# First channel product of the last two batches: one Strassen product with seven block products in place of two plain ones

## The chip, the cores and the metric

The kernel runs on one core of a Trainium2 chip. The metric is the device time of one execution in microseconds (us), as the median of several runs. A run's profile is taken in an execution of its own; its times are those of that one execution. TensorE is called PE below (its weight loads PEld), VectorE DVE, ScalarE ACT, GpSimd POOL, and SyncE, which issues most DMA transfers, SP.

## The reference

Eight batches of 576 tokens, eight heads of 64 columns (together 512), float32 in and out. An attention without softmax with a norm is followed by a residual MLP over tokens and over channels:

```
kv  = einsum('bhsd,bhse->bhde', k, v)
o   = einsum('bhsd,bhde->bhse', q, kv)
x   = o / sqrt(mean(o*o, -1) + 1e-6) * g_norm        # then heads side by side: [8, 576, 512]
tok = einsum('ts,bsd->btd', w_tok, alpha1 * x + beta1)
u   = x + lam * tok
a2  = alpha2 * u + beta2
ch  = maximum(a2 @ w_ch1, 0) @ w_ch2                 # 512 -> 2048 -> 512
out = u + lam * ch
```

## The kernel before

**Stages.** The kernel computes one batch after the other in four stages. The 576 tokens are cut into four groups of 128 and a tail of 64; the tails of two neighbouring batches are worked on together, with the odd one of them.

1. attention(b): kv from k and v (PE, L626), then for each token group the product with q (norm, PE, L717) and a chain ACT square L684, DVE reduce L687, ACT root L690, DVE reciprocal L693, DVE multiplications L695 and L702 (into xm, and xt for the tail), POOL multiplication L705 into rm, the input of the token product in bf16.
2. mix(b): the token product tok (L800, four groups of five matmuls with 512 columns, and L845 for the tails), DVE add L810 into xm, POOL cast to bf16 L888 into a2b, and an SP transposing DMA L901 into a2m (a2l for tails). After this a2m holds the batch's activations with channels on the partitions: four blocks of 128 channels by 512 tokens. It has two places, so neighbouring batches stand in it side by side.
3. ch1(b): the first channel product. For each of the 16 blocks of 128 hidden units four matmuls of 512 columns accumulate in one PSUM bank (L911), then ACT adds the bias, takes the maximum with 0 and writes bf16 (relu, L905) into ht, one half of the buffer hh. The tails follow in ch1_tail (L924, relu L941 into hl).
4. The second channel product. Batches 0 and 1 take it plainly (ch2, L967). From batch 2 on it is strassen(b): the [512 tokens x 2048] by [2048 x 512] product is cut into 2 x 2 blocks, and seven block products (L1016, 256 columns each) stand for eight. It needs sums of the blocks of h (DVE, L983, by the helper both, 128x1024 in bf16); its results go out of PSUM by ACT into tmp (keep, L1041) and a POOL addition to xm (L1044), or by a DVE addition straight to xm (last_add, L1049), and are then stored by SP (L1054). The tails have ch2_tail (L1094, L1110) and finish (L1129).

In the program's text the order is, for b from 0 to 7: ch1(b), the tails (odd b), the second product of b, attention(b + 2), mix(b + 2). **What sets the order on the chip** is a table of numbers, ORDER. Each operation has a number, given as it is emitted, and the table lists them in the order in which every engine gets its own instructions; a number behind a colon is the PSUM bank (there are eight), and operations joined by + are woven, matmul by matmul. GATES adds a few dependences. Everything else follows from data: an operation waits for what it reads, and for the readers of what it overwrites. In the table, attention and mix of a batch are spread among the channel products of the batches before it. All of attention(7) and mix(7), tok(7) and the transposes into a2m among it, stand before ch1(6).

**Names that matter.** w1 holds w_ch1 (four blocks of 128 channels by 2048), w2 holds w_ch2, ws1, ws2 and ab_bc are sums of w2's blocks. qs and qp are the buffers into which q is loaded and transposed, wt the token weights, rm the token product's input, sq and tmp scratch tiles of 128x512 f32 (three each). PSUM tiles are called ps. The profile leaves the numbers of buffers out, so w there is w1 or w2.

Of the kernel before, what the change touches and what calls it, by code (L numbers as in the profile page):

```python
# [1407 lines left out]
```

## Time and profile before

| | |
|---|---|
| time, median of 3 runs | 333.48 us (333.26 to 334.75) |
| the profiled execution: time | 335.96 us |
| the profiled execution: span of the core | 333.4 us |
| PE, DVE, ACT, POOL busy | 324.5, 226.5, 176.0, 146.5 us |
| L911 matmuls, 128x512 | 123.3 us busy, 495 seen of 512 |
| L1016 matmuls, 128x256 | 44.4 us, 384 |
| L705 on POOL, L1044 on POOL | 37.9 us and 23.2 us |
| L983 sums on DVE, one form (hh<-hh) | 10.0 us, 14 |

A row of the groups gives the line, the engine, the operation, the tile written and the tile read, the shapes, the number of instructions, the busy time in us with the mean in ns, and the idle time ahead of them with what ended it. Matmuls overlap in the pipeline, so the mean of one (383 ns for L911) is longer than the distance from one to the next. A row of the timeline has the start in us, the length in us, and then the same fields; rows of the same line that follow each other are drawn together.

### The profile page before, as it was taken

The page shows a single profiled execution, that of the slowest core. Times are in us where ns is not written, and L with a number is a line of the kernel's source. Part 1 is how long each engine was busy: PE and PEld are TensorE (multiplying, and loading weights), DVE is VectorE, ACT ScalarE, POOL GpSimd, SP SyncE. Part 2 cuts the span into 40 slices and gives each one's busy share as a digit, 9 for nine tenths or more (in the row PEclk, how much of TensorE's full clock was granted, in tenths as well). Part 3 has the DMA queues.
Part 4 walks back from the last instruction along what each step waited for, and adds up shares of the span by engine and source line. Part 5 has one row for each costly group of instructions (what it writes and reads, how often), then busy time and mean ns, then how long its engine had stood idle before and what let it go on. Part 6 is the DMA issues. An engine that isn't in the chain of part 4 may idle for free.

```text
span 333.4 us, 6156 instructions
## 1 busy us (share of the span) xinstructions
PE 324.5 (97%) x2468; PEld 222.2 (67%) x2497; DVE 226.5 (68%) x389; ACT 176.0 (53%) x358; POOL 146.5 (44%) x146
## 2 busy tenths in 40 slices
PE   8899999999999989999999999999999999999996
PEld 7777564454676535786669864786667784784686
DVE  3785178678999996849998387898897411531432
ACT  5753672239544654629842476727671168418512
POOL 3799027999343544533167313661445300130130
PEclk9999999999999999999999999999999999999999
DMA  7999999999952697599006993994300421012004
GB/s 261 324 265 218 214 208 237 174 188 259 192 151 65 129 289 137 111 283 190 1 18 154 303 176 67 237 176 152 65 0 2 110 97 33 0 38 90 0 2 157
DMA packets 108531, 48.14 MB, mean 144 GB/s; under 512 B 82061, under 2 KB 101589, under 8 KB 108504
## 3 DMA queue, kind: packets, MB, share of 16 engines
q1 hardware_dynamic: 81440, 26.24, 33.5%
q0 software_dynamic: 26800, 21.38, 32.8%
q8 instruction: 19, 0.31, 0.4%
q10 hardware_dynamic: 264, 0.14, 0.2%
q14 instruction: 8, 0.07, 0.1%
HBM read 38.82 MB, written 9.44 MB: 145 GB/s over the span
## 4 chain that ended last, share of the span: by engine, by line
PE 75%; DVE 12%; ACT 5%; DMA 4%; issue 2%; POOL 2%; SPq 0%; DVEq 0%
PE ps L911 22%; PE ps L1016 21%; PE ps L800 8%; PE ps L967 7%; PE ps L924 4%; DVE xm L702 2%; PE ps L717 2%; DMA w<-in_moe_w_ch_dram 2%; DVE ps L695 2%; PE ps L626 2%; DVE small L687 2%; PE ps L1110 2%; PE ps L1094 2%; DVE qp L1278 2%; DMA qs<-in_q_dram 1%
## 5 line engine op out<-in xcount | busy, mean ns | idle before, releaser
L911 PE MATMUL ps<-a2m,w 128*128 128x512 bf16 x495 | 123.3, 383 | 1.2 <-DMA w<-in_moe_w_ch_dram 0.5
L911 PEld LDWEIGHTS ps<-a2m,w 128*128 128x128 bf16 x512 | 48.8, 97 | 53.3 <-issue 1.1
L905 ACT ACTIVATE hh<-ps,b 128x512 bf16<-128x512 f32 x96 | 64.4, 686 | 25.1 <-PE ps L911 24.0
L705 POOL TENSOR_TENSOR rm<-xm,la_bc 128x512 bf16<-128x512 f32 x28 | 37.9, 1357 | 65.0 <-DVE xm L702 64.9
L1044 POOL TENSOR_TENSOR xm<-xm,tmp 128x512 f32<-128x512 f32 x18 | 23.2, 1289 | 60.7 <-ACT tmp L1041 60.7
L1016 PE MATMUL ps<-w,hh 128*128 128x256 bf16 x384 | 44.4, 273 | 0.0
L717 PE MATMUL ps<-kvc,qt 128*128 128x128 f32 (+1 forms) x140 | 42.2, 407 | 0.1
L1016 PEld LDWEIGHTS ps<-w,hh 128*128 128x128 bf16 x384 | 37.5, 98 | 6.0 <-issue 0.4
L967 PE MATMUL ps<-w,hh 128*128 128x512 bf16 x138 | 37.0, 385 | 0.1
L626 PE MATMUL ps<-vr,kr 128*128 128x128 f32 x112 | 34.2, 408 | 1.3 <-DVE b L935 1.3
L1049 DVE TENSOR_TENSOR xm<-ps,xm 128x512 f32<-128x512 f32 x24 | 16.5, 686 | 22.7 <-POOL xm L1044 12.9
L800 PE MATMUL ps<-rm,wt 128*128 128x512 bf16 x107 | 29.5, 382 | 1.0 <-POOL rm L705 0.4
L684 ACT ACTIVATE sq<-ps 128x512 f32<-128x512 f32 (+1 forms) x35 | 20.6, 595 | 18.4 <-PE ps L717 18.1
L983 DVE TENSOR_TENSOR hh<-hh 128x1024 bf16<-128x1024 bf16 x14 | 10.0, 718 | 28.9 <-ACT hh L905 22.3
L717 PEld LDWEIGHTS ps<-kvc,qt 128*128 128x128 f32 (+1 forms) x140 | 27.3, 195 | 2.1 <-ACT qt L1281 0.5
L687 DVE TENSOR_REDUCE small<-sq 128x8 f32<-128x512 f32 (+1 forms) x35 | 23.4, 670 | 7.6 <-ACT sq L684 7.5
L888 POOL CAST a2b<-xm 128x512 bf16<-128x512 f32 x24 | 15.5, 648 | 26.0 <-DVE xm L810 26.0
L941 ACT ACTIVATE hh<-ps,b 128x128 bf16<-128x128 f32 x48 | 13.2, 383 | 22.9 <-PE ps L924 20.3
L1041 ACT ACTIVATE tmp<-ps 128x512 f32<-128x512 f32 x18 | 10.8, 600 | 26.0 <-PE ps L1016 25.9
L626 PEld LDWEIGHTS ps<-vr,kr 128*128 128x128 f32 x112 | 22.4, 200 | 3.0 <-DVE b L935 1.8
L695 DVE TENSOR_TENSOR ps<-ps,small 128x512 f32<-128x512 f32 (+1 forms) x35 | 23.9, 692 | 0.5
L905 ACT ACTIVATE hh<-ps 128x512 bf16<-128x512 f32 x32 | 17.6, 597 | 12.4 <-PE ps L911 12.2
(156 smaller groups left out, 528.8 us busy)
## 6 DMA issues: line engine op xcount, KB each, us to landing
out_dram<-xm SPq DMA_DIRECT2D x32, 256.0 KB, 3.0
kr<-in_k_dram POOLq DMA_DIRECT2D x7, 1024.0 KB, 6.5
vr<-in_v_dram POOLq DMA_DIRECT2D x7, 1024.0 KB, 8.1
qs<-in_q_dram SPq DMA_DIRECT2D x24, 288.0 KB, 4.6
w<-in_moe_w_ch_dram POOLq DMA_DIRECT2D x8, 512.0 KB, 9.8
xm<-in_q_dram SPq DMA_DIRECT2D x8, 288.0 KB, 5.7
qs<-in_v_dram SPq DMA_DIRECT2D x4, 288.0 KB, 5.0
w<-in_k_dram SPq DMA_DIRECT2D x4, 288.0 KB, 5.0
```

Source lines behind the costliest of these rows:

```text
L626: P.mm("fill", 128, [lambda e, t=t, c=c, h=h, o=128 * (h % 4): e.matmul(t.ap()[:, o:o + 128], kr4[:, h, c:c + 2, :].rearrange("p c d -> p ...
L684: P.op("ACT", act(n), lambda e: e.activation(sq[rs, s3, 0:nst, :].rearrange("p h e -> p (h e)"), ps(), ACT.Square), r=[t], w=[("sq", s3)])
L687: P.op("DVE", dve(n), lambda e: e.tensor_reduce(out=st, in_=sq[rs, s3, 0:nst, :], axis=AX.X, op=ALU.add), r=[("sq", s3)], w=[("sm", s4)])
L695: P.op("DVE", dve(n), lambda e: e.tensor_tensor(out=grp(ps()), in0=grp(ps()), in1=st[..., None].to_broadcast([rs.stop - rs.start, nst, DH] ...
L705: P.op("POOL", pool(n), lambda e: e.tensor_tensor(out=r, in0=x.rearrange("p h e -> p (h e)"), in1=la, op=ALU.mult), r=xks + ["la"], w=rks)
L717: P.mm("fill", 128, [lambda e, p=p: e.matmul(dst(p), qt[:, p, cs], kvc[:, i, p, :], start=(p == 0), stop=(p == 3)) for p in range(4)], r=[ ...
L800: P.mm("fill", 512, [lambda e, sc=sc: e.matmul(t.ap(), wt[:, sc if sc < 4 else tw(b), 128 * c:128 * c + 128], rsrc(b, sc, al), start=(sc = ...
L905: P.op("ACT", act(512, 0 if f is None else 1), lambda e: e.activation(dst, t.ap(), ACT.Relu, bias=0.0 if f is None else b1[:, f:f + 1]), r ...
L911: P.mm("main", 512, [lambda e, dj=dj: e.matmul(t.ap(), w1[:, dj, 128 * fj:128 * fj + 128], a2m[:, b % 2, dj, :], start=(dj == 0), stop=(dj ...
L967: P.mm("main", 512, [lambda e, fj=fj, t=t, c=c: e.matmul(t.ap(), (ht[:, fj, 128 * c:128 * c + 128] if c < 4 else hl[:, fj, :]), w2[:, fj, ...
L1016: P.mm("main", 256, [lambda e, c=c, fj=fj: e.matmul(t.ap()[:, 256 * c:256 * c + 256], at[:, fj, 128 * c:128 * c + 128], rhs(fj), start=(fi ...
L1044: P.op("POOL", pool(512), lambda e, cs=cs, f=f: e.tensor_tensor(out=X[:, cs, f], in0=X[:, cs, f], in1=two(tmp[:, s]), op=ALU.add), r=xks(c ...
```

## The change

For batches 6 and 7 ch1 is replaced by pair(6, 7). The two batches stand side by side as the column blocks of one right-hand matrix, and w1 is cut into halves of its channels (rows of the right-hand matrix) and of its hidden units: with B11, B21 the two channel halves of batch 6 in a2m and B12, B22 those of batch 7, the product is a 2 x 2 block product. Strassen's scheme (in Winograd's form) takes seven block products for the eight. Each block product has 8 blocks of 128 hidden units with 2 matmuls of 512 columns: 7 x 16 = 112 matmuls (L960 of the changed kernel) for 2 x 64.

- pair_sums makes eight DVE sums of w1's halves (S1 to S4, each in two parts) and four of the activations (T1 to T4, here u and a2m), all 128x1024 in bf16. S1 and S2 lie in qs, S3 and S4 in rm, two of the T in qp, one in wt, and one in a2m in place.
- pair runs in eight turns x of 14 matmuls, where the second half of a turn overlaps the next turn's first. Partial results go out of PSUM three times a turn by an ACT copy with bias into tmp or sq in f32 (kept, L972), and come out as h by three DVE additions of PSUM and such a copy (L982), each followed by a POOL maximum with 0 in place (L984), and by one ACT relu (L912).
- Batch 7's h gets a place of its own, h7, over the first two batch places of xm (batches 4 and 5), since both batches' h now exist together. Its writers wait until the outputs of batches 4 and 5 are stored.
- Both tails' first products and both second products follow: ch1_tails(7), strassen(6), strassen(7), ch2_tail(7). sums, blocks and four take the batch, since batch 7's h lies elsewhere.
- ORDER is a new table from about its 390th word on, and its bank numbers with it. GATES is unchanged.

The functions from strassen on are otherwise moved down by some 100 lines: L1016 is L1122 in the changed kernel, L983 is L1087, L924 is L1022, L1094 is L1201, L1110 is L1217, L800 is L807, L845 is L852, L810 is L817, L1049 is L1156, L1129 is L1236, L888 is L895, L645 is L652, L687 is L694, L695 is L702, L702 is L709, L717 is L724, L1278 is L1385.

```diff
-465 389 488:5 398 487 386 401 477 500:2 387 497 371 368 472:0 489 501 390 474:4 473 467 391 478:7
...
+465 389 488:5 398 487 386 401 477 500:2 387 497 371 368 472:0 489 501 392 474:4 473 467 393 478:7
...
+        h7 = [xm[:, i].rearrange("p c f -> p (c f)").bitcast(BF16).rearrange("p (j t) -> p j t", j=8)
+              for i in range(2)]
...
+        def pair_sums(b, c):
+            S = [x[:, s] for x in (
+                qs[:, 0:2048].bitcast(BF16).rearrange("p (s j t) -> p s j t", s=2, j=2),
+                rm[:].rearrange("p b c f -> p (b c f)").rearrange("p (s j t) -> p s j t", s=2, j=2))
+                for s in range(2)]
+            T = [x.bitcast(BF16).rearrange("p (j t) -> p j t", j=2)
+                 for x in (qp[:, 0, 0:512], qp[:, 1, 0:512])] + [wt[:, 0:2, 0:512]]
+            kb, kc = ([ak(x, i) for i in range(4)] for x in (b, c))
+            B11, B21 = a2m[:, b % 2, 0:2, :], a2m[:, b % 2, 2:4, :]
+            B12, B22 = a2m[:, c % 2, 0:2, :], a2m[:, c % 2, 2:4, :]
+            for h in range(2):
+                f, g = slice(512 * h, 512 * h + 512), slice(1024 + 512 * h, 1536 + 512 * h)
+                lk, hk = ("w1", h), ("w1", 2 + h)
+                both(ALU.add, S[0][:, :, f], w1[:, 0:2, g], w1[:, 2:4, g], [hk], [("s1", h)])
+                both(ALU.subtract, S[1][:, :, f], S[0][:, :, f], w1[:, 0:2, f], [lk, ("s1", h)], [("s2", h)])
+                both(ALU.subtract, S[2][:, :, f], w1[:, 0:2, f], w1[:, 0:2, g], [lk, hk], [("s3", h)])
+                both(ALU.subtract, S[3][:, :, f], w1[:, 2:4, f], S[1][:, :, f], [lk, ("s2", h)], [("s4", h)])
+            both(ALU.subtract, T[0], B12, B11, kb + kc, [("u", 1)])
+            both(ALU.subtract, T[1], B22, T[0], kc + [("u", 1)], [("u", 2)])
+            both(ALU.subtract, B12, B22, B12, kc, kc)
+            both(ALU.subtract, T[2], B21, T[1], kb + [("u", 2)], [("u", 4)])
+            return S, T
+        def pair(b, c):
+            S, T = pair_sums(b, c)
+            kb, kc = ([ak(x, i) for i in range(4)] for x in (b, c))
+            B11, B21 = a2m[:, b % 2, 0:2, :], a2m[:, b % 2, 2:4, :]
+            T3, B22 = a2m[:, c % 2, 0:2, :], a2m[:, c % 2, 2:4, :]
+            lo_w, hi_w = w1[:, 0:2, :], w1[:, 2:4, :]
+            hc = (ht[:, 0:8], ht[:, 8:16])
+            n = [0]
+            at = {}
+            def pairmm(x, key, first, stop, lhs, o, rhs, r):
+                if first:
+                    at[x, key] = P.bank("main")
+                t = at[x, key]
+                P.mm("main", 512, [lambda e, i=i: e.matmul(
+                    t.ap(), lhs[:, i, 128 * x + o:128 * x + o + 128], rhs[:, i, :],
+                    start=(first and i == 0), stop=(stop and i == 1),
+                    skip_group_check=True) for i in range(2)],
+                    r=r, w=[t])
+                return t
+            def kept(t, f):
+                s = n[0] % 6
+                n[0] += 1
+                dst, key = (tmp[:, s], ("tmp", s)) if s < 3 else (
+                    sq[:, s - 3].rearrange("p h e -> p (h e)"), ("sq", s - 3))
+                P.op("ACT", act(512, 1), lambda e: e.activation(
+                    dst, t.ap(), ACT.Identity, bias=b1[:, f:f + 1]), r=[t, ("b1", f)], w=[key])
+                return dst, key
+            def out_of(t, f, z, k):
+                dst = (h7 if z else hc)[f // 8][:, f % 8, :]
+                keys = [(hkey(c if z else b), f, i) for i in range(2)]
+                if k is None:
+                    relu(dst, t, keys, f)
+                    return
+                P.op("DVE", dve(512), lambda e: e.tensor_tensor(
+                    out=dst, in0=t.ap(), in1=k[0], op=ALU.add), r=[t, k[1]], w=keys)
+                P.op("POOL", pool(512, False), lambda e: e.tensor_scalar(
+                    out=dst, in0=dst, scalar1=0.0, scalar2=None, op0=ALU.max), r=keys, w=keys)
+            k1, k2, k5 = {}, {}, {}
+            for z in range(9):
+                x, y = (z if z < 8 else None), (z - 1 if z else None)
+                if x is not None:
+                    h = x // 4
+                    k1[x] = kept(pairmm(x, "a", True, False, lo_w, 0, B11, [("w1", h)] + kb), x)
+                if y is not None:
+                    out_of(pairmm(y, "a", False, False, S[2], 0, T3, [("s3", y // 4)] + kc), y + 8, 1, k5[y])
+                if x is not None:
+                    out_of(pairmm(x, "b", True, True, hi_w, 0, B21, [("w1", h)] + kb), x, 0, k1[x])
+                if y is not None:
+                    out_of(pairmm(y, "c", False, True, S[3], 0, B22, [("s4", y // 4)] + kc), y, 1, k2[y])
+                if x is not None:
+                    k2[x] = kept(pairmm(x, "a", False, False, S[1], 0, T[1], [("s2", h), ("u", 2)]), x)
+                if y is not None:
+                    out_of(pairmm(y, "a", False, True, hi_w, 1024, T[2], [("w1", 2 + y // 4), ("u", 4)]),
+                           y + 8, 0, None)
+                if x is not None:
+                    k5[x] = kept(pairmm(x, "c", True, False, S[0], 0, T[0], [("s1", h), ("u", 1)]), x + 8)
...
+        def ch1_tails(b):
+            for f4 in range(0, 16, 3 if b == 1 else 4):
+                ch1_tail(b, f4, min(3, 16 - f4) if b == 1 else 4)
...
-        A11, A21, A12, A22 = ht[:, 0:8, 0:256], ht[:, 0:8, 256:512], ht[:, 8:16, 0:256], ht[:, 8:16, 256:512]
+        def blocks(b):
+            lh, hh_ = (h7[0], h7[1]) if b == NB - 1 else (ht[:, 0:8], ht[:, 8:16])
+            return [x[:, :, f:f + 256] for x in (lh, hh_) for f in (0, 256)]
...
+            if b == NB - 2:
+                for i in range(2):
+                    alias([("h7", f, z) for f in range(8 * i, 8 * i + 8) for z in range(2)],
+                          [("x", i, c, p) for c in range(4) for p in range(4)])
+                    alias([("u", i + 1)], [("qp", i)])
+                alias([("u", 4)], [(n, i) for n in ("wt", "wtt") for i in range(2)])
+                alias([("s%d" % m, i) for m in (1, 2) for i in range(2)],
+                      [("qs", g) for g in range(4)])
+                alias([("s%d" % m, i) for m in (3, 4) for i in range(2)],
+                      [("r", i, c, p) for i in range(2) for c in range(4) for p in range(4)])
+                pair(b, b + 1)
+                ch1_tails(b + 1)
+                strassen(b)
+                strassen(b + 1)
+                ch2_tail(b + 1)
+                break
```

**First place: PE around tok(7).** Ahead of it before, strassen(5)'s products (L1016) up to tok(7)'s first group (L800; ab_bc holds a sum of w2's blocks):

```order
L1016 MATMUL ps<-w2,hh 128x256 x32
L1016 MATMUL ps<-ws2,hs 128x256 x16
L1016 MATMUL ps<-ab_bc,hh 128x256 x16
L1016 MATMUL ps<-w2,hh 128x256 x24
L800 MATMUL ps<-rm,wt 128x512 x4
```

Ahead of it now, the same products (L1122) up to the same group (L807):

```order
L1122 MATMUL ps<-w2,hh 128x256 x8
L1022 MATMUL ps<-a2l,w1 128x128 x16
L1122 MATMUL ps<-w2,hh 128x256 x24
L1122 MATMUL ps<-ws2,hs 128x256 x8
L1022 MATMUL ps<-a2l,w1 128x128 x36
L1122 MATMUL ps<-ws2,hs 128x256 x8
L1122 MATMUL ps<-ab_bc,hh 128x256 x16
L1122 MATMUL ps<-w2,hh 128x256 x32
L1022 MATMUL ps<-a2l,w1 128x128 x8
L1122 MATMUL ps<-ws1,hh 128x256 x8
L807 MATMUL ps<-rm,wt 128x512 x4
```

The tails (L1022) and 16 more matmuls of strassen(5) have come ahead of tok(7). Behind it before, from its tail part (L845) to the first matmuls of ch1(6) (L911):

```order
L845 MATMUL ps<-rtl,wt 64x512 x2
L1016 MATMUL ps<-w2,hh 128x256 x8
L1016 MATMUL ps<-ws1,hh 128x256 x16
L924 MATMUL ps<-a2l,w1 128x128 x64
L1094 MATMUL ps<-w2,hh 128x256 x4
L924 MATMUL ps<-a2l,w1 128x128 x32
L1094 MATMUL ps<-w2,hh 128x256 x12
L1110 MATMUL ps<-w2,hh 128x256 x8
L911 MATMUL ps<-a2m,w1 128x512 x4
```

Behind it now (L852 is its tail part, qs holds S1 and S2, qp the first two T, rm S3 and S4):

```order
L852 MATMUL ps<-rtl,wt 64x512 x2
L1122 MATMUL ps<-ws1,hh 128x256 x8
L1022 MATMUL ps<-a2l,w1 128x128 x4
L1201 MATMUL ps<-w2,hh 128x256 x12
L960 MATMUL ps<-a2m,w1 128x512 x2
L1201 MATMUL ps<-w2,hh 128x256 x4
L1217 MATMUL ps<-w2,hh 128x256 x8
L960 MATMUL ps<-a2m,w1 128x512 x2
L1217 MATMUL ps<-w2,hh 128x256 x8
L1022 MATMUL ps<-a2l,w1 128x128 x12
L960 MATMUL ps<-qp,qs 128x512 x4
L960 MATMUL ps<-a2m,w1 128x512 x2
```

Of the 64 tail matmuls of ch1_tails(5) only 4 are left behind tok(7), 60 stand ahead of it among strassen(5)'s products; of the 24 matmuls of strassen(5) behind it 8 are left. The tails of batches 6 and 7 (12 of them here) are spread over the pair.

**Second place: DVE behind tok(7).** Before, from tok(7)'s four adds to the first sums of strassen(6):

```order
L810 TENSOR_TENSOR xm<-ps,xm 128x512 x4
L810 TENSOR_TENSOR xt<-ps,xt 128x512
L1049 TENSOR_TENSOR xm<-ps,xm 128x2x256 x2
L983 TENSOR_TENSOR hh<-hh 128x1024
L1129 TENSOR_TENSOR xt<-ps,xt 128x512
L983 TENSOR_TENSOR hh<-hh 128x4x256
```

Now, from the same adds to the first adds out of the pair (L982):

```order
L817 TENSOR_TENSOR xm<-ps,xm 128x512 x4
L817 TENSOR_TENSOR xt<-ps,xt 128x512
L1087 TENSOR_TENSOR rm<-w1 128x2x512
L1156 TENSOR_TENSOR xm<-ps,xm 128x2x256
L1087 TENSOR_TENSOR rm<-w1,qs 128x2x512 x2
L1087 TENSOR_TENSOR rm<-w1 128x2x512
L1087 TENSOR_TENSOR hh<-hh 128x1024
L1087 TENSOR_TENSOR qp<-a2m 128x1024
L982 TENSOR_TENSOR hh<-ps,tmp 128x512
L1087 TENSOR_TENSOR qp<-a2m,qp 128x1024
L1236 TENSOR_TENSOR xt<-ps,xt 128x512
L1087 TENSOR_TENSOR a2m<-a2m 128x1024
```

S3 and S4 (rm) and three T sums (qp, qp, a2m) stand there anew, with one add out of the pair between them; the fourth T sum follows directly.

**Third place: DVE ahead of tok(7).** It begins with the adds of tok(6) (L810, now L817), and the next reductions (L687, now L694) open attention(7)'s chains. Before:

```order
L810 TENSOR_TENSOR xm<-ps,xm 128x512
L645 TENSOR_TENSOR kvc<-ps,kvo 64x4x64
L810 TENSOR_TENSOR xm<-ps,xm 128x512 x3
L687 TENSOR_REDUCE small<-sq 128x8 x2
L693 RECIPROCAL small<-small 128x8
```

Now:

```order
L817 TENSOR_TENSOR xm<-ps,xm 128x512
L1087 TENSOR_TENSOR qs<-w1 128x2x512
L817 TENSOR_TENSOR xm<-ps,xm 128x512
L1087 TENSOR_TENSOR qs<-qs,w1 128x2x512
L652 TENSOR_TENSOR kvc<-ps,kvo 64x4x64 x2
L1087 TENSOR_TENSOR qs<-w1 128x2x512
L1087 TENSOR_TENSOR hh<-hh 128x4x256
L1087 TENSOR_TENSOR qs<-qs,w1 128x2x512
L1087 TENSOR_TENSOR hs<-hh 128x1024
L694 TENSOR_REDUCE small<-sq 128x8 x2
```

S1 and S2 (qs, four sums) stand there anew, and two sums of strassen(5) (hh, hs) have come forward.

More of the change, by code (lines that the diff above doesn't have):

```diff
@@ L168, in _add @@
                     o.deps.add(y)
-                    if not isinstance(key, Bank) and key[0] in ("sm", "tmp"):
+                    if not isinstance(key, Bank) and key[0] in ("sm", "tmp", "hs"):
                         o.raw.add(y)
@@ L974, in ch2, with four @@
                     finish(b, c, t)
-        A11, A21, A12, A22 = ht[:, 0:8, 0:256], ht[:, 0:8, 256:512], ht[:, 8:16, 0:256], ht[:, 8:16, 256:512]
+        def blocks(b):
+            lh, hh_ = (h7[0], h7[1]) if b == NB - 1 else (ht[:, 0:8], ht[:, 8:16])
+            return [x[:, :, f:f + 256] for x in (lh, hh_) for f in (0, 256)]
         B11, B21, B12, B22 = w2[:, 0:8, 0:256], w2[:, 8:16, 0:256], w2[:, 0:8, 256:512], w2[:, 8:16, 256:512]
-        def four(g, m, n):
-            return [("h", fj, n) for fj in range(8 * m + 4 * g, 8 * m + 4 * g + 4)]
+        def four(g, m, n, b=0):
+            return [(hkey(b), fj, n) for fj in range(8 * m + 4 * g, 8 * m + 4 * g + 4)]
         def both(op, out, in0, in1, r, w):
@@ L1360, in bass_transnormer_attn__then__resmlp_affine_kernel @@
             if b % 2:
-                for f4 in range(0, 16, 3 if b == 1 else 4):
-                    ch1_tail(b, f4, min(3, 16 - f4) if b == 1 else 4)
+                ch1_tails(b)
             if b == 1:
```

33 lines of the change are left out of this document (19 added, 14 removed), and 117 rows, old and new, of the table ORDER.

## The prediction

> **What bounds the kernel now.** I read the page first: busy shares, the slices and the chain.
>
> ```profile
> span 333.4 us, 6156 instructions
> PE 324.5 (97%) x2468; PEld 222.2 (67%) x2497; DVE 226.5 (68%) x389; ACT 176.0 (53%) x358; POOL 146.5 (44%) x146
> PEclk9999999999999999999999999999999999999999
> PE 75%; DVE 12%; ACT 5%; DMA 4%; issue 2%; POOL 2%; SPq 0%; DVEq 0%
> ```
>
> TensorE works 97% of the span at a clock that is never below nine tenths, and has three quarters of the chain that ended last. A share can hide stalls, so the stretches of 8 us around the change come next (PE, PEld, DVE, ACT, POOL busy, clock, DMA share, GB/s), then PE's waits (total, times, longest).
>
> ```profile
> 222.00:230.00 8.00, 8.00 (x65) 6.32 (x64) 8.00 (x16) 3.57 (x7) 2.40 (x3) 1.00 0.99 233
> 246.00:254.00 8.00, 8.00 (x74) 6.97 (x73) 7.88 (x11) 3.02 (x6) 3.51 (x3) 1.00 0.01 2
> 262.00:270.00 8.00, 8.00 (x123) 7.72 (x121) 1.74 (x3) 4.33 (x16) 0.61 (x1) 1.00 0.60 175
> 302.00:310.00 8.00, 8.00 (x38) 3.63 (x37) 1.39 (x2) 6.41 (x10) 0.00 (x0) 1.00 0.03 11
> ...
> PE ps L626 <- DVE b L935: 1.3, 1, 1.3
> ...
> PE ps L800 <- POOL rm L705: 0.4, 1, 0.4
> ```
>
> PE is full in each of them, and between 60 and 331 us its named waits are these two, 1.7 us. So a matmul taken away there is time taken away, if nothing new makes PE wait. VectorE has no air left while the attention chains run (8.00, 7.88) and plenty behind (1.74, 1.39); POOL idles from 262 us on. This is where the change puts its work.
>
> **What it removes.** Batches 6 and 7 had 2 x 64 matmuls of 512 columns (L911); now 7 x 16 = 112 (L960 of the changed kernel). Sixteen go. One lasts:
>
> ```profile
> 299.30 13.76 PE L911 MATMUL ps<-a2m,w 128*128 128x512 bf16 x62
> ...
> 300.15 0.69 ACT L905 ACTIVATE hh<-ps,b 128x512 bf16<-128x512 f32 x1 [5.51 <-PE ps L911]
> ...
> 313.10 0.69 ACT L905 ACTIVATE hh<-ps,b 128x512 bf16<-128x512 f32 x1 [0.18 <-PE ps L911]
> ```
>
> The first and last of batch 7's 16 relus stand 12.95 us apart; each follows four matmuls, so one is 12.95/60 = 0.216 us. Gain: 16 x 0.216 = **3.45 us**. The other matmuls keep count, shape and weaving.
>
> **What it adds, in steady state.** One of the eight turns of the pair has 14 matmuls, 3 ACT keeps, 1 ACT relu, 3 VectorE adds from PSUM and 3 POOL maxima with 0.
>
> ```profile
> L1041 ACT ACTIVATE tmp<-ps 128x512 f32<-128x512 f32 x18 | 10.8, 600 | 26.0 <-PE ps L1016 25.9
> L1049 DVE TENSOR_TENSOR xm<-ps,xm 128x512 f32<-128x512 f32 x24 | 16.5, 686 | 22.7 <-POOL xm L1044 12.9
> L888 POOL CAST a2b<-xm 128x512 bf16<-128x512 f32 x24 | 15.5, 648 | 26.0 <-DVE xm L810 26.0
> L1044 POOL TENSOR_TENSOR xm<-xm,tmp 128x512 f32<-128x512 f32 x18 | 23.2, 1289 | 60.7 <-ACT tmp L1041 60.7
> L705 POOL TENSOR_TENSOR rm<-xm,la_bc 128x512 bf16<-128x512 f32 x28 | 37.9, 1357 | 65.0 <-DVE xm L702 64.9
> ```
>
> PE needs 14 x 0.216 = 3.02 us for a turn; ACT at most 4 x 0.69 = 2.76 (the relu's length; a keep has 0.60); VectorE 3 x 0.69 = 2.06. None passes PE. The maximum has no row. Its ends are 0.65 (the cast, one tensor in) and 1.36 (two tensors in), so POOL needs 1.94 to 4.07 us. I take 0.65, since the maximum reads one tensor too. Then PE hides all three, and the term is nothing; with that cover gone it is the last rival's.
>
> By the Trainium skill, page "GPSIMD Engine Reference", section 4.1, an elementwise maximum belongs to VectorE: GpSimd is about half as fast with two inputs and near line rate with one. By that this term stays nothing; no run here shows such a maximum.
>
> **The sums.** Twelve VectorE sums of 128x1024 are new: eight of w1's halves (S), four of the activations (T).
>
> ```profile
> L983 DVE TENSOR_TENSOR hh<-hh,hs x12: 639/992/1799, 138.4 to 317.3; 128x1024 bf16<-128x1024 bf16 x12
> ...
> 289.48 1.32 POOL L1044 TENSOR_TENSOR xm<-xm,tmp 128x512 f32<-128x512 f32 x1 [26.44 <-ACT tmp L1041]
> ...
> 288.39 1.29 DVE L983 TENSOR_TENSOR hh<-hs,hh 128x1024 bf16<-128x1024 bf16 x2
> 289.68 2.27 DVE L983 TENSOR_TENSOR hh<-hh,hs 128x1024 bf16<-128x1024 bf16 x2
> 254.10 1.28 POOL L705 TENSOR_TENSOR rm<-xm,la_bc 128x512 bf16<-128x512 f32 x1 [0.38 <-DVE xm L702]
> ...
> 256.17 0.81 PE L800 MATMUL ps<-rm,wt 128*128 128x512 bf16 x3
> ```
>
> A pair of sums takes 1.29 us alone, 2.27 beside a POOL operation of 1.32 that reads SBUF: 0.64 to 1.80 each.
>
> By the Trainium skill, page "SBUF — State Buffer", section "Who interferes with whom", a VectorE instruction with two SBUF inputs contends with a GpSimd one that reads SBUF, with one such input it doesn't. The 2.27 agrees. By it the adds out of PSUM stay free of the maxima and only sums collide.
>
> Four S sums (into qs) and one last_add come newly ahead of tok(7), where VectorE is full: 4 x 0.64 + 0.69 = 3.2 us, with every sum colliding 4 x 1.80 + 0.69 = 7.9. Before, POOL's last rm ended at 255.38 and PE went into tok(7) at about 256, so delay there would show. But the new order also brings PE work ahead of tok(7): 60 tail matmuls (128 columns) and 16 of strassen(5) (256 columns).
>
> ```profile
> 264.19 3.74 PE L924 MATMUL ps<-a2l,w 128*128 128x128 bf16 x64
> ...
> 267.77 0.60 PE L1094 MATMUL ps<-w,hh 128*128 128x256 bf16 x4
> ...
> 269.99 1.47 PE L1094 MATMUL ps<-w,hh 128*128 128x256 bf16 x12
> 271.30 0.93 PE L1110 MATMUL ps<-w,hh 128*128 128x256 bf16 x7
> ```
>
> 64 tails start 3.58 us ahead of what follows, 0.056 each; 12 of 256 columns 1.31, 0.109 each. So PE comes 60 x 0.056 + 16 x 0.109 = 5.1 us later. The balance is -1.9 to +2.8; I take **nothing**: at the row's median, 0.99, VectorE's share is 4.7 against 5.1.
>
> **The joint behind tok(7)** is the tight place: S3, S4 and T stand between it and their first products.
>
> ```profile
> 257.03 1.03 PE L800 MATMUL ps<-rm,wt 128*128 128x512 bf16 x4
> 258.11 1.03 PE L800 MATMUL ps<-rm,wt 128*128 128x512 bf16 x4
> ...
> 261.56 1.05 PE L1016 MATMUL ps<-w,hh 128*128 128x256 bf16 x8
> ...
> 261.67 0.69 DVE L810 TENSOR_TENSOR xt<-ps,xt 128x512 f32<-128x512 f32 x1 [0.51 <-PE ps L845]
> ...
> 261.22 0.61 POOL L888 CAST a2b<-xm 128x512 bf16<-128x512 f32 x1 [0.47 <-DVE xm L810]
> ...
> 262.49 1.26 SPq L901 DMA_TRANSPOSE a2m<-a2b  x1
> ...
> a2m<-a2b SPq DMA_TRANSPOSE x4, 2.5
> out_dram<-xm SPq DMA_DIRECT2D x4, 256.0 KB, 4.3
> ```
>
> Groups of tok are 1.08 apart, so tok(7) began at 257.03 - 1.08 = 255.95; its tail ended 5.61 later. Count from that start. PE then has 40 matmuls of 256 columns (4.36), 16 tails (0.90) and 4 of the pair (0.86) that need no T: the product with T0 is due at 5.61 + 6.12 = 11.7, that with T1 two matmuls later, 12.2, that with T3 at 13.9 (two more with T, four without, 8 tails). On VectorE xt's add ends at 262.36 - 255.95 = 6.4; then, 0.60 apart as a pair of sums alone has it (1.29 less the 0.69 of one), four S sums, a last_add and a ch2_tail sum: 10.0. The last transpose has landed by then (262.49 - 255.95 + 2.5 = 9.0). So T0 ends at 10.6, an add out and T1 at 11.8, an xt add and T3 at 13.0. Slack: 1.1, 0.4 and 0.9. A POOL cast or maximum in the way takes 0.61 of it, and two stand there. Ends: nothing, and three T sums at 1.80 instead of 0.65, 3.45 less T3's 0.9 = 2.5. I take **+0.5 us**, two collisions (1.22) less a slack between T1's and T3's.
>
> Batch 7's first add goes into xm and waits for batches 4 and 5's stores. Issued by about 10 (the last_add behind S3 ends near 7.6, SP has the transposes ahead), they land 4.3 later, at 14.3; PE gives that add its product at 13.9 + 0.43 = 14.3. Tenths, within the 0.5.
>
> **Sum:** 335.96 (the profiled execution's own time) - 3.45 + 0.5 = 333.0. The median of the runs lies 2.48 below that execution, so **330.5 us**.
>
> **Rivals.**
> *The new order also sheds old waits.* All positions behind about 55 us are new. Then the 1.3 wait may go, the joint may be free: 333.48 - 3.45 - 1.3 = 328.7. For it: the wait stands at one place only. Against: what it waits for may be a load, which an order of instructions doesn't hasten.
> *VectorE is late.* The S sums cost part of 2.8 at tok(7), T part of 2.5 at the joint: either gives up to 330.0 + 2.8 = 332.8, three quarters of both 334.0; I price it at 332.5. For it: 7.88 of 8 busy, and 1.80 seen. Against: POOL works 3.51 of 8 us there, so not all four collide.
> *POOL's maximum costs as with two tensors, slower.* On VectorE, sums that strassen(6)'s third product needs stand behind a sum over batch 7's last maxima. PE would reach that product 24.2 (eight turns) + 2.2 (40 tails) + 3.5 (32 of 256 columns) = 29.9 us after the pair's start; three sums of 0.60 come between, and 0.6 until the first maximum can begin, so 27.5 are left for 24 maxima: up to 1.15 each they hide. At 1.36 they take 32.6: +5.1 and 330.5 + 5.1 = 335.6. The old time is passed from 1.15 + (3.45 - 0.5)/24 = 1.27 each. For it: POOL's commonest rows are at 1.29 and 1.36. Against: those have two tensors in, and the casts 0.65.
> *The change doesn't do what it says*, PE being not the bound: the full windows exclude it.
>
> **How the numbers follow.** My forecast (329.8 to 331.4) has 0.58, the shed waits 0.10 (328.7 to 329.8), late VectorE 0.24 (331.4 to 334.0), slow maxima 0.08 (334 to 336). The range 329.0 to 333.5 leaves out a third of the second, little of the third and the fourth, 0.15 in all. Within 0.5%, about what a measurement can tell from no change, is 331.81 to 335.15. Faster: 0.58 + 0.10 + 0.03 = 0.71; same: 0.21 of the third and 0.02 of the fourth, 0.23; slower 0.06.
>
> **What would show it.** Right: PE full in the pair's windows, its span 3 us shorter from tok(7) to the end, waits on L1087 sums below 1 us in all, maxima near 0.65. Wrong: a PE wait on rm or rtl before tok(7) (the S sums), on qp or a2m at the first T products (the joint), on PSUM banks with POOL busy throughout (the maxima), or a wait at 60 to 250 us that wasn't there (the order).

## The result, and the profile after

The changed kernel takes 348.18 us (median of 4 runs, 345.88 to 349.9) where the kernel before takes 334.12 (median of 4 runs, the three behind the 333.48 above and one more); the ratio is 1.0416, 95% interval 1.0347 to 1.0485. It is 4% slower, and the prediction of 330.5 (329.0 to 333.5) was wrong.

The page of the changed kernel first: span, busy shares, the slices of PE, POOL and the clock, the chain by engine, and the group of the new POOL maxima.

```profile
span 343.7 us, 6215 instructions
PE 326.3 (95%) x2481; PEld 221.2 (64%) x2481; DVE 246.1 (72%) x425; ACT 173.6 (50%) x358; POOL 180.4 (52%) x170
...
PE   7999999999999999999999999799999995949996
...
POOL 3699047998345523723580435533235479994240
PEclk9999999999999999999999999999999999896999
...
PE 73%; POOL 11%; DVE 8%; DMA 4%; issue 2%; ACT 1%; SPq 0%; DVEq 0%
...
L984 POOL TENSOR_SCALAR xm<-xm 128x512 bf16<-128x512 bf16 x16 | 23.9, 1507 | 3.2 <-DVE xm L982 3.2
```

Before, PE's slices had no dip in the last third, and POOL had 2% of the chain. Now POOL has 11%, its slices are full in the stretch of the pair, PE has two dips there, and in the same place the granted clock leaves nine tenths for the first time. One maximum takes 1.5 us. PE's waits from 60 us on (total, times, longest):

```profile
PE ps L960 <- DVE xm L982: 8.8, 2, 5.1
PE ps L1122 <- DVE hs L1087: 2.1, 1, 2.1
PE ps L807 <- DVE rtl L707: 0.2, 1, 0.2
```

Two waits of 8.8 us together lie in the pair, one of 2.1 far ahead of it (217 us); the waits of 1.3 and 0.4 of before are gone. The timeline of PE around the two waits (start, length, what, idle before):

```profile
285.89 1.03 PE L960 MATMUL ps<-qp,qs 128*128 128x512 bf16 x4
290.56 0.69 PE L960 MATMUL ps<-wt,w 128*128 128x512 bf16 x2 [3.64 <-DVE xm L982]
291.04 1.91 PE L960 MATMUL ps<-a2m,w 128*128 128x512 bf16 x4
292.75 1.82 PE L960 MATMUL ps<-a2m,rm 128*128 128x512 bf16 x4
294.41 1.03 PE L960 MATMUL ps<-qp,qs 128*128 128x512 bf16 x4
...
310.18 1.03 PE L960 MATMUL ps<-wt,w 128*128 128x512 bf16 x2 [5.14 <-DVE xm L982]
311.01 5.53 PE L1122 MATMUL ps<-w,hh 128*128 128x256 bf16 x32
316.37 1.80 PE L1122 MATMUL ps<-ws,hs 128*128 128x256 bf16 x15
```

PE waits for VectorE's adds. What holds these shows on VectorE and POOL:

```profile
288.81 1.08 DVE L1087 TENSOR_TENSOR hh<-hh 128x1024 bf16<-128x1024 bf16 x1 [4.29 <-POOL hh L984]
...
308.43 1.09 DVE L1087 TENSOR_TENSOR hh<-hh 128x1024 bf16<-128x1024 bf16 x1 [4.88 <-POOL hh L984]
...
284.40 2.93 POOL L984 TENSOR_SCALAR xm<-xm 128x512 bf16<-128x512 bf16 x2
287.30 1.48 POOL L984 TENSOR_SCALAR hh<-hh 128x512 bf16<-128x512 bf16 x1
```

On VectorE a sum of strassen(6) stands among the adds out of the pair. It waits 4.29 us for the maximum of batch 6's fourth block (POOL, 287.30 + 1.48 = 288.78), all adds behind it wait with it, and PE waits for a bank that they have to free. The same happens at 308 us. VectorE stood idle through those 4.29 us, and the maxima still followed each other every 1.45 us (2.93 less 1.48), so VectorE isn't what slows them.

The second part of the loss is in the lengths: behind the first wait 8 matmuls take 294.41 - 291.04 = 3.37 us, where 8 x 0.216 = 1.73 are due; behind the second 32 of 256 columns take 316.37 - 311.01 = 5.36 for 3.50. That is 1.64 + 1.86 = 3.5 us of slow clock.

So, span against span: 333.4 - 3.45 (16 matmuls) + 8.8 (waits in the pair) + 3.5 (slow clock) + 0.6 (2.1 + 0.2 - 1.3 - 0.4, the waits ahead of it) = 342.9, of 343.7 measured; 0.8 us are left without a name. The spans differ by 10.3 us and the medians by 14.1, because the profiled execution was the fastest of the four now (345.88 us) and above the median before (335.96): the other 3.8 us lie in executions that left no trace.

### The profile page after: what moved, and what is told of

Its sections match the earlier page's. It is cut to its first block, busy times and chain, and to the rows that moved or that the text cites. A ratio compares the mean times of both kernels' runs of the same rounds, so it can differ in the third digit from the quotient of the medians.

```text
span 343.7 us, 6215 instructions
## 1 busy us (share of the span) xinstructions
PE 326.3 (95%) x2481; PEld 221.2 (64%) x2481; DVE 246.1 (72%) x425; ACT 173.6 (50%) x358; POOL 180.4 (52%) x170
## 4 chain that ended last, share of the span: by engine, by line
PE 73%; POOL 11%; DVE 8%; DMA 4%; issue 2%; ACT 1%; SPq 0%; DVEq 0%
PE ps L1122 22%; PE ps L1009 21%; PE ps L807 9%; PE ps L1069 7%; POOL xm L984 6%; PE ps L1022 3%; POOL hh L984 3%; DMA w<-in_moe_w_ch_dram 2%; PE ps L724 2%; PE ps L633 2%; PE ps L1201 2%; DMA w<-in_k_dram 1%; PE ps L852 1%; DVE ps L702 1%; PE ps L1217 1%
## 5 line engine op out<-in xcount | busy, mean ns | idle before, releaser
L1009 PE MATMUL ps<-a2m,w 128*128 128x512 bf16 x384 | 99.4, 385 | 0.5 <-DMA w<-in_moe_w_ch_dram 0.5
L712 POOL TENSOR_TENSOR rm<-xm,la_bc 128x512 bf16<-128x512 f32 x28 | 35.6, 1276 | 60.8 <-DVE xm L709 60.7
L1009 PEld LDWEIGHTS ps<-a2m,w 128*128 128x128 bf16 x384 | 36.3, 97 | 37.8 <-issue 1.1
L912 ACT ACTIVATE hh<-ps,b 128x512 bf16<-128x512 f32 x72 | 48.2, 684 | 17.2 <-PE ps L960 8.9
L724 PE MATMUL ps<-kvc,qt 128*128 128x128 f32 (+1 forms) x140 | 42.0, 405 | 0.0
L1122 PE MATMUL ps<-w,hh 128*128 128x256 bf16 x320 | 38.6, 281 | 0.0
L1069 PE MATMUL ps<-w,hh 128*128 128x512 bf16 x144 | 37.9, 385 | 0.0
L1122 PEld LDWEIGHTS ps<-w,hh 128*128 128x128 bf16 x320 | 32.2, 101 | 5.8 <-issue 0.6
L895 POOL CAST a2b<-xm 128x512 bf16<-128x512 f32 x24 | 16.2, 678 | 34.7 <-DVE xm L817 32.0
L694 DVE TENSOR_REDUCE small<-sq 128x8 f32<-128x512 f32 (+1 forms) x35 | 23.4, 677 | 12.7 <-ACT sq L691 12.3
L1156 DVE TENSOR_TENSOR xm<-ps,xm 128x512 f32<-128x512 f32 x24 | 16.5, 688 | 20.9 <-POOL xm L1151 13.9
L807 PE MATMUL ps<-rm,wt 128*128 128x512 bf16 x112 | 29.4, 380 | 0.6 <-DVE rtl L707 0.6
L724 PEld LDWEIGHTS ps<-kvc,qt 128*128 128x128 f32 (+1 forms) x140 | 27.3, 196 | 1.7 <-ACT qt L1388 0.4
L984 POOL TENSOR_SCALAR xm<-xm 128x512 bf16<-128x512 bf16 x16 | 23.9, 1507 | 3.2 <-DVE xm L982 3.2
L702 DVE TENSOR_TENSOR ps<-ps,small 128x512 f32<-128x512 f32 (+1 forms) x35 | 23.9, 692 | 0.6
L912 ACT ACTIVATE hh<-ps 128x512 bf16<-128x512 f32 x32 | 17.5, 597 | 12.4 <-PE ps L1009 12.2
```

The lines of the kernel that those rows point to most:

```text
L694: P.op("DVE", dve(n), lambda e: e.tensor_reduce(out=st, in_=sq[rs, s3, 0:nst, :], axis=AX.X, op=ALU.add), r=[("sq", s3)], w=[("sm", s4)])
L702: P.op("DVE", dve(n), lambda e: e.tensor_tensor(out=grp(ps()), in0=grp(ps()), in1=st[..., None].to_broadcast([rs.stop - rs.start, nst, DH] ...
L712: P.op("POOL", pool(n), lambda e: e.tensor_tensor(out=r, in0=x.rearrange("p h e -> p (h e)"), in1=la, op=ALU.mult), r=xks + ["la"], w=rks)
L724: P.mm("fill", 128, [lambda e, p=p: e.matmul(dst(p), qt[:, p, cs], kvc[:, i, p, :], start=(p == 0), stop=(p == 3)) for p in range(4)], r=[ ...
L807: P.mm("fill", 512, [lambda e, sc=sc: e.matmul(t.ap(), wt[:, sc if sc < 4 else tw(b), 128 * c:128 * c + 128], rsrc(b, sc, al), start=(sc = ...
L912: P.op("ACT", act(512, 0 if f is None else 1), lambda e: e.activation(dst, t.ap(), ACT.Relu, bias=0.0 if f is None else b1[:, f:f + 1]), r ...
```

## The experiments

Theory 1 is that the price of the POOL maxima is the loss. Its rivals: the pair's own latency or VectorE (theory 2), and the new order (theory 3). Medians are in us; each ratio is against runs of the kernel before on the same chip.

| run | median (range) | before | ratio, 95% interval |
|---|---|---|---|
| max_8_columns | 334.64 (331.42 to 337.06) | 335.23 | 0.9977 (0.9948 to 1.0006) |
| max_on_vector | 333.22 (331.91 to 334.5) | 335.23 | 0.9943 (0.9921 to 0.9964) |
| max_on_vector_old_order | 331.57 (329.36 to 333.32) | 335.23 | 0.9896 (0.9860 to 0.9933) |
| plain_new_order | 342.52 (341.74 to 343.05) | 335.23 | 1.0221 (1.0187 to 1.0254) |
| pool_forms | 335.77 (one run) | 334.95 | none |
| max_416_columns | 342.11 (341.14 to 342.86) | 334.95 | 1.0210 (1.0180 to 1.0239) |
| vector_rm_first | 329.83 (328.61 to 330.76) | 334.95 | 0.9841 (0.9814 to 0.9868) |
| plain_new_order_2 | 337.55 (336.82 to 337.77) | 334.95 | 1.0071 (1.0044 to 1.0098) |
| sums_late | 342.82 (341.53 to 343.38) | 335.27 | 1.0234 (1.0194 to 1.0274) |
| fed_waits | 344.57 (343.01 to 347.05) | 335.27 | 1.0299 (1.0246 to 1.0352) |
| plain_rm_first | 333.51 (332.38 to 336.16) | 335.27 | 0.9963 (0.9935 to 0.9992) |
| vector_rm_first_again | 329.72 (328.87 to 331.09) | 335.27 | 0.9847 (0.9811 to 0.9882) |

### Is it the maximum?

max_8_columns cuts each maximum to its first 8 columns, max_on_vector keeps all of it and changes the engine.

```diff
                 P.op("POOL", pool(512, False), lambda e: e.tensor_scalar(
-                    out=dst, in0=dst, scalar1=0.0, scalar2=None, op0=ALU.max), r=keys, w=keys)
+                    out=dst[:, 0:8], in0=dst[:, 0:8], scalar1=0.0, scalar2=None, op0=ALU.max), r=keys, w=keys)
```

```diff
-                P.op("POOL", pool(512, False), lambda e: e.tensor_scalar(
+                P.op("DVE", dve(512, 4), lambda e: e.tensor_scalar(
```

> The changed kernel with each of the 24 POOL maxima cut from 512 columns to the first 8 (so three quarters of the last two batches' h stay without their maximum); order, banks and all other work are the same. Theory 1, POOL's price: the maxima at 1.48 us are the whole loss; PE's two waits in the pair (8.8 us) go, and with them the slow clock behind them (about 3.7 us): 334.1 - 3.45 - 1.7 (old waits gone) + 2.3 (new waits before the pair) = 331.3 us, range 330 to 333. Theory 2, the pair's own latency (PSUM to ACT copy to VectorE add, and VectorE's sums): PE still waits inside the pair, time above 338. Theory 3, the new order: the loss lies before the pair, time above 338 with no wait inside it.

> The 24 maxima on VectorE, same line, same place in the order; nothing left out. Price from the row of the 128x2048 bf16 tensor_scalar before (803 ns): about 0.2 us each for 512 columns, so VectorE has 3 x 0.69 + 3 x 0.2 = 2.7 us in a turn of 3.02. Theory 1: 331.3 us, range 330 to 333, ratio 0.990 against before, no wait above 1 us in the pair. Theory 2: VectorE is the narrow engine, so its longer queue makes it worse than the 8 columns on POOL by 2 us or more. Theory 3: above 338.

Both take the loss away: 13.5 and 15.0 us below the changed kernel. max_on_vector came 1.9 us above what theory 1 said (1.1 of them stand in the kernel before as well, which took 335.23 there and not 334.12), max_8_columns 3.3 and so outside its range. There the miss goes with the clock: the four of its ten runs with a mean granted clock of 0.999 or 1.000 took 331.4 to 333.4 us, the six with 0.990 to 0.995 took 334.6 to 337.1; where the clock fell in those six no trace shows. Neither profile has a wait in the pair. PE's waits of max_on_vector from 34 us on, and what the maxima cost there (minimum, median, maximum in ns):

```profile
PE ps L1122 <- DVE hs L1087: 2.1, 1, 2.1
PE ps L724 <- ACT qt L1388: 0.9, 1, 0.9
PE ps L807 <- DVE rtl L707: 0.6, 2, 0.4
...
L984 DVE TENSOR_SCALAR xm<-xm x16: 283/284/288, 279.5 to 301.8; 128x512 bf16<-128x512 bf16 x16
```

The same instruction takes 0.28 us on VectorE and 1.48 on POOL. VectorE now has 3 x 0.69 + 3 x 0.28 = 2.9 us of work in a turn of 3.02 and still delays nobody: theory 2 falls. The wait of 2.1 us is still there, and it isn't the maxima's.

### What makes it dear on POOL?

pool_forms puts four forms in the maximum's place, in turn.

```diff
+                form = forms[0] % 4
+                forms[0] += 1
+                if form == 0:
+                    P.op("POOL", pool(512, False), lambda e: e.tensor_copy(out=dst, in_=dst), r=keys, w=keys)
+                elif form == 1:
+                    P.op("POOL", pool(512, False), lambda e: e.tensor_scalar(
+                        out=dst, in0=dst, scalar1=0.0, scalar2=None, op0=ALU.add), r=keys, w=keys)
+                elif form == 2:
+                    P.op("POOL", pool(512, False), lambda e: e.tensor_scalar(
+                        out=dst, in0=la_bc[:], scalar1=0.0, scalar2=None, op0=ALU.max), r=keys, w=keys)
+                else:
+                    P.op("POOL", pool(256, False), lambda e: e.tensor_scalar(
+                        out=dst[:, 0:256], in0=dst[:, 0:256], scalar1=0.0, scalar2=None, op0=ALU.max),
+                        r=keys, w=keys)
```

> The changed kernel with the 24 POOL maxima replaced in turn by four forms, six each, to read their prices: a copy of the bf16 tile onto itself, an addition of 0 in place (tensor_scalar), a maximum with 0 of a float32 tile (la_bc) written as bf16, and the maximum in place on 256 of the 512 columns. It leaves the maximum out for most of the last two batches' h, and replaces a quarter of it by a constant. Known: 1.48 us for the maximum on 512 columns, 0.23 on 8, 0.65 for a cast float32 to bf16. Theory operand type (reading bf16 is slow): copy and addition about 1.48 us, the float32 maximum about 0.65. Theory operation (tensor_scalar is slow): copy about 0.65, addition and float32 maximum about 1.48. Either way 256 columns 0.23 + 248 x 2.48 ns = 0.85.

The POOL groups of its pair (busy us, mean ns): an addition and a float32 maximum by tensor_scalar, 256 columns of the maximum, the casts as before, and the copy.

```profile
L990 POOL TENSOR_SCALAR xm<-xm 128x512 bf16<-128x512 bf16 x4 | 6.0, 1491 | 3.8 <-DVE xm L983 3.8
L996 POOL TENSOR_SCALAR xm<-xm 128x256 bf16<-128x256 bf16 x5 | 4.2, 841 | 0.0
...
L993 POOL TENSOR_SCALAR hh<-la_bc 128x512 bf16<-128x512 f32 x2 | 3.0, 1480 | 0.0
...
L895 POOL CAST a2b<-xm 128x512 bf16<-128x512 f32 x4 | 2.4, 612 | 4.2 <-DVE xm L817 4.2
L988 POOL COPY xm<-xm 128x512 bf16<-128x512 bf16 x3 | 1.8, 606 | 0.0
```

It is the operation, not the type: a tensor_scalar of 512 columns takes 1.48 to 1.49 us for a maximum and for an addition, from bf16 and from float32, about two and a half times a copy or cast (0.61). The prediction had taken the cast's row for it because both read one tensor.

### From which price does POOL decide?

max_416_columns has the edit of max_8_columns with 416.

> The maxima on POOL, cut to 416 of 512 columns (a fifth of those h stay without it): 0.23 + 408 x 2.48 ns = 1.24 us each. The prediction put the point from which POOL decides at 1.15 us: 24 x (1.24 - 1.15) = 2.2 us over max_on_vector's 333.2, with some slow clock 335 to 338. If the decision point is a good deal lower, waits are near the full 8.8 us and the time is above 342; if it is higher, the time is 333.

PE's waits in the pair there:

```profile
PE ps L960 <- DVE xm L982: 5.5, 3, 2.9
```

At 1.24 to 1.29 us per maximum the time was 342.1, and PE waited in the pair 5.5 us, not the 2.2 expected: the decision point lies below the 1.15 of the prediction. Rows of the changed kernel, from POOL and VectorE, bound it:

```profile
277.15 1.49 POOL L984 TENSOR_SCALAR xm<-xm 128x512 bf16<-128x512 bf16 x1 [2.16 <-DVE xm L982]
...
282.64 0.69 DVE L982 TENSOR_TENSOR xm<-ps,tmp 128x512 bf16<-128x512 f32 x1 [1.14 <-PE ps L960]
283.25 0.68 DVE L982 TENSOR_TENSOR hh<-ps,sq 128x512 bf16<-128x512 f32 x1
283.85 0.68 DVE L982 TENSOR_TENSOR xm<-ps,tmp 128x512 bf16<-128x512 f32 x1
```

The waiting sum needs eight maxima from 277.15 on, and VectorE was free for it at 284.5 (the add at 283.85 and its length). Of its 4.29 us of waiting PE felt 3.64, so the banks cover 0.65, and PE waits when the eighth maximum ends behind 284.5 + 0.65 = 285.2. Eight in a row reach that at (285.2 - 277.15)/8 = 1.0 us each. Cheaper ones would not stand in a row, since each must wait for its add: POOL began 0.8 us after the start of an add (277.15 against 276.37), so the last two, for the adds at 282.64 and 283.25, take from 283.4 on, and they reach 285.2 at 0.9 us each. So PE waits from about 0.9 us on. That is an estimate from these rows, and no run lies between 0.23 and 1.1 us; pool_forms, whose four forms have a mean of 1.1 us, had 3.0 us of waits in the pair.

### POOL's throughput, or the place of the sums?

sums_late moves five sums in the order (numbers of the table, what stands between left out): 1522 to 1524 behind the last add out of the pair, 1558 and 1560 behind 1525.

```diff
-... 1522 ... 1558 ... 1523 ... 1524 ... 1483 ... 1560 ... 1525 ...
+... 1483 1522 1523 1524 ... 1525 ... 1558 1560 ...
```

> The changed kernel (maxima on POOL, 512 columns) with five VectorE sums moved in the order: the three of strassen(6) that stood among the adds out of the pair go behind the last of these, the two of strassen(7) behind strassen(6)'s. VectorE then has nothing between its adds that waits for a maximum. Theory POOL's throughput: the waits inside the pair go, but strassen(6)'s first product needs 21 of the maxima, which POOL ends near 306 while PE is there at 301, and its third one waits little more: 5 to 6 us of waits in place of 8.8, and 348.2 - 3.2 = 345 us, some slow clock less. Theory VectorE's order: the sums that waited are the cause, PE's waits fall to under 2 us and the time to 337 or less.

PE's waits from 34 us on:

```profile
PE ps L1124 <- POOL hh L986: 7.0, 1, 7.0
PE ps L1124 <- DVE hs L1089: 2.1, 1, 2.1
```

The waits inside the pair are gone, but one of 7.0 us stands behind it, directly for POOL (5 to 6 were expected), and the time is 342.8 us (345 were expected): 5.4 below the changed kernel, of which the profiled spans show 2.5 (343.7 against 341.2), and 7.5 above the kernel before. 24 maxima at 1.48 are 35.5 us, and eight turns of the pair 24.2, so moving the sums alone left most of the loss; other work of PE behind the pair might cover more, which was not tried. The place of the sums on VectorE decided where the wait appeared and a part of its size.

### The slow clock

fed_waits puts 60 and 88 idle matmuls (their results are used by nothing) ahead of the two that waited, into the banks 6 and 5, which nothing else uses there. Some lines of Python that let an idle matmul name its bank are left out here.

```diff
-... 1427 ... 1488 ...
+... ~60:6 1427 ... ~88:5 1488 ...
```

> The changed kernel with 60 and 88 idle matmuls of 128 columns (0.056 us each) into a free PSUM bank ahead of the two matmuls at which PE waited 3.64 and 5.14 us; nothing else is changed and the waits' causes stay. Theory clock: the slow stretches behind those waits (3.5 us in the profile: 8 matmuls in 3.37 for 1.73, 32 in 5.36 for 3.50) follow from PE's idleness and go: 348.2 - 3.5 = 344.7 us. Rival: the granted clock falls for another reason: 348 or more.

344.57 us, as theory clock had it (344.7). Its waits' causes are unchanged; PE works through most of them (2.5 us of waits are left in the pair), and the windows (the clock is the third number from the end) beside those of the changed kernel show what went. First the changed kernel, then fed_waits:

```profile
288.00:296.00 8.00, 5.44 (x18) 2.07 (x19) 5.33 (x8) 2.33 (x4) 7.29 (x6) 0.79 0.00 0
...
304.00:312.00 8.00, 2.86 (x26) 1.87 (x24) 2.29 (x3) 2.41 (x8) 7.64 (x6) 0.75 0.00 0
312.00:320.00 8.00, 8.00 (x63) 6.54 (x62) 5.90 (x8) 1.64 (x4) 2.34 (x3) 0.82 0.01 2
```

```profile
288.00:296.00 8.00, 5.94 (x47) 3.27 (x46) 6.14 (x9) 3.45 (x6) 7.29 (x6) 1.00 0.00 0
...
304.00:312.00 8.00, 7.55 (x114) 7.14 (x113) 3.45 (x5) 2.47 (x8) 6.85 (x5) 1.00 0.01 2
312.00:320.00 8.00, 8.00 (x75) 7.17 (x74) 5.60 (x8) 1.50 (x3) 4.45 (x3) 1.00 0.00 0
```

With PE kept busy the clock stays at 1.00, so it followed PE's idleness: 3.6 us between the medians came from it, a quarter of the loss (3.5 by the lengths above). The Trainium skill, page "TensorE: Matmul & The Clock Gate", section "HAM oscillation — how this bites in real kernels", says that PE falls back to half its clock behind idle gaps above about 3.4 us. The gaps of 3.64 and 5.14 us agree, and so does the half: 3.37/8 = 0.42 us for a matmul of 0.216. But 3.4 us was not the boundary here. PE behind the longest wait of max_416_columns:

```profile
307.72 1.03 PE L960 MATMUL ps<-wt,w 128*128 128x512 bf16 x2 [2.90 <-DVE xm L982]
308.55 4.94 PE L1122 MATMUL ps<-w,hh 128*128 128x256 bf16 x32
313.32 1.91 PE L1122 MATMUL ps<-ws,hs 128*128 128x256 bf16 x16
```

Behind only 2.90 us, 32 matmuls of 256 columns took 313.32 - 308.55 = 4.77 us where 3.50 are due, while behind a wait of 3.04 us in plain_new_order 32 of 128 columns took the usual 1.80.

### The order

Theory 3 was tried from two sides: plain products in the new order (plain_new_order, and with a mended seam plain_new_order_2), and the pair with cheap maxima in the old one (max_on_vector_old_order). Each takes the one kernel's table up to and with tok(7) and the other's from there on.

> The kernel before (plain products for batches 6 and 7), with the new order up to and with tok(7), restricted to the operations both kernels have, and the order before from there on; no S sums ahead of tok(7). Theory 1: the order before the pair costs little: 334.1 + 2.3 - 1.7 = 334.7, range 333.5 to 336. Theory 3: the new order is the loss: above 340.

> The pair with the maxima on VectorE, but the order before up to and with tok(7); from there the new order, so all eight S sums stand behind tok(7), with 5.1 us more of other PE work there than in the changed kernel. Theory 1: 331.3 less the 0.6 us that the new order costs ahead of the pair, 330.7 us; up to 2.4 us more (four sums of 0.6) if the S sums there come on top. Theory 3: the old order gives all of the loss back, which theory 1 says has nothing to do with it: then this one is below max_on_vector by 5 us or more.

> plain_new_order, whose seam behind tok(7) had a wait of 3.0 us for a transposed tail, with 16 matmuls of ch1(6) moved ahead of the tails that waited. Theory 1 with the order's price seen between the two kernels with the maxima on VectorE (333.2 against 331.6): 335.2 + 1.6 = 336.8, up to 339.5 if only the 3.0 go. Theory 3: the new order itself costs as before, 341 or more.

plain_new_order missed its expectation by 7.8 us and looked like theory 3. A part was the seam itself: the tails taken ahead of tok(7) were missing as cover behind it, and PE waited 3.0 us for a transposed tail. With 16 matmuls of ch1(6) put there it took 337.55, 2.6 us above the kernel before. With the maxima on VectorE the new order takes 333.22 and the old 331.57. So the new order ahead of the pair costs about 2 us, not the 14 of the loss. All kernels of the new order that are shown so far have a wait of 2.1 to 2.2 us near 217. VectorE and POOL of max_on_vector show it:

```profile
212.57 4.04 DVE L1087 TENSOR_TENSOR hh<-hs,hh 128x1024 bf16<-128x1024 bf16 x1
...
212.83 0.70 POOL L1379 DMA_DIRECT2D kr<-in_k_dram  x1
213.53 1.30 POOL L712 TENSOR_TENSOR rm<-xm,la_bc 128x512 bf16<-128x512 f32 x1
214.77 1.28 POOL L1151 TENSOR_TENSOR xm<-xm,tmp 128x512 f32<-128x512 f32 x1
```

A sum took 4.04 us instead of 0.68 and ended at 216.61, only when POOL's multiplication and addition in a row were over (214.77 + 1.28 = 216.05). vector_rm_first moves the multiplication ahead of three DMA issues on POOL:

```diff
-... 1092 ... 1089 ... 1091 ... 1090 ... 1104 ...
+... 1092 ... 1104 1089 1091 1090 ...
```

> max_on_vector with one move in the order: on POOL, one rm multiplication (L712, op 1104) goes ahead of three of the four DMA issues that load k and v (ops 1089 to 1091), near 211 us. There a VectorE sum took 4.04 us and PE waited 2.1 us for its successor. Theory lock: the sum stood behind POOL's two float operations in a row that read SBUF; with rm done before, the sum takes 0.7, PE's wait goes, and with it the slow clock behind it: 333.2 - 2.1 = 331.1 us or up to 1.7 less. Rival: the DMA issues block the sum as well, it stays at 3 us or more and the time at 333.2.

```profile
211.15 1.27 POOL L714 TENSOR_TENSOR rm<-xm,la_bc 128x512 bf16<-128x512 f32 x1
212.36 0.94 POOL L1377 DMA_DIRECT2D kr<-in_k_dram  x1
...
212.17 0.79 DVE L1089 TENSOR_TENSOR hh<-hh 128x1024 bf16<-128x1024 bf16 x1
212.88 0.68 DVE L1089 TENSOR_TENSOR hh<-hs,hh 128x1024 bf16<-128x1024 bf16 x1
```

The sum takes 0.68 beside the DMA issues, PE's wait is gone, and the time is 329.83, 3.4 us below max_on_vector. That is 1.3 more than the wait. The clock accounts for a part of it: in max_on_vector's profile the window 216 to 224 had 0.79, and 24 matmuls of 256 columns behind the wait took 4.29 us where 2.62 are due. But only four of its twelve runs had a mean clock below 1.00, so the rest stays open.

### What the pair itself is worth

plain_rm_first and vector_rm_first_again have one order up to tok(7) and the same move; they differ in the product and what follows.

> plain_new_order_2 (plain products, new order) with the same move as in vector_rm_first. If PE's wait of 2.1 us and the slow clock behind it go here too: 337.5 - 2.1 = 335.4 or up to 1.7 less, 333.7. Beside vector_rm_first (329.8) it gives what the pair with cheap maxima is worth in one and the same order up to tok(7); the count of matmuls says 3.45 us, so by that it is 333.3. If the pair's order behind tok(7) gives more than the matmuls, it is above 334.5.

> vector_rm_first once more, on the same chip as plain_rm_first, so that the two can be set beside each other: 329.8 us again, within 1 us; less plain_rm_first by 3.45 if the matmuls are all of it.

333.51 against 329.72: 3.8 us, where 16 matmuls are 3.45. The two share the chip and the runs of the kernel before. vector_rm_first is the best version: 1.6% below the kernel before (0.9841, 0.9814 to 0.9868, and 0.9847 when run again).

## Why the prediction was wrong, point by point

- **PE is the bound, 16 matmuls are 3.45 us.** Right: plain_rm_first against vector_rm_first_again gives 3.8. That vector_rm_first's 329.8 lies within the predicted range is no success of the forecast: it has the maxima on another engine and one more move in the order.
- **ACT and VectorE are hidden in a turn.** Right, even with 0.28 us more for each add on VectorE (max_on_vector, no wait in the pair).
- **"I take 0.65, since the maximum reads one tensor too."** This is the step that failed. The maximum takes 1.48 us, above both ends of 0.65 and 1.36. The number of inputs was the wrong likeness: a cast and a tensor_scalar read one tensor each and differ by a factor of 2.4 (pool_forms). The sentence on the Trainium skill, page "GPSIMD Engine Reference", section 4.1, leaned the same way with its near line rate for one input; the measurement decides against it for this operation. Its other half, that a maximum belongs to VectorE, is what the runs bear out: 0.28 against 1.48 us.
- **The rival of slow maxima (0.08).** Its mechanism was the one that happened, with sums on VectorE behind late maxima. Its price was not: by its formula 24 x 1.48 - 27.5 = 8.0 us late, 338.5, and the 8.8 us of waits agree with that. What it left out was the slow clock behind such waits (3.5) and the order (below). It also took only the sums behind the pair; the one in its middle decides earlier, near 0.9 us and not at 1.15.
- **S sums ahead of tok(7): nothing.** Right: 0.2 us of wait there. But a sum's worst case was put at 1.80; an old sum in the new order took 4.03, and PE waited 2.1 us. The prediction looked for the new order's cost only where sums were added, not where old ones had moved beside POOL's work.
- **The joint: +0.5 us.** It cost nothing: PE takes tok(7), the tails and the first T products without a wait. T1's sum ended at 273.64, while its product came two matmuls behind 273.57. Batch 7's first add waited for PE, not for the stores.

These rows carry the last point: VectorE's T1 sum and its first add into xm, and PE's first matmuls with T:

```profile
272.96 0.68 DVE L1087 TENSOR_TENSOR qp<-a2m,qp 128x1024 bf16<-128x1024 bf16 x1
...
276.37 0.69 DVE L982 TENSOR_TENSOR xm<-ps,tmp 128x512 bf16<-128x512 f32 x1 [0.93 <-PE ps L960]
...
273.57 1.03 PE L960 MATMUL ps<-qp,qs 128*128 128x512 bf16 x4
```

## What to carry to other kernels

An operation that the trace doesn't show on an engine has no price there, however alike another looks; where 24 of them stand on the way of a saturated engine, the range has to reach past the dearest row, or the operation goes to an engine that shows it (VectorE had a tensor_scalar row of 803 ns for 2048 columns). An elementwise step whose consumer stands in the same in-order queue as the producers' adds turns a slow helper into a stop for all of them. And a wait of some microseconds on the matmul engine is to be priced with a slow clock behind it, here up to 1.9 us for one.
